# A streaming decode attention kernel: the critical section synchronised from GpSimd, and the last V blocks summed in three pieces instead of two

## The chip, the cores and the metric

The kernel runs on one core of one Trainium2 chip. Its time is the device time of one execution in microseconds (us).

## The reference, cut to what matters

```
# one token; x is [1, 1, 448]; 16 query heads, 8 KV heads, 65536 cached positions, head size 256
q = (x @ wq) -> 16 heads
scores = q . k_cache * 256 ** -0.5 ;  p = softmax(scores) ;  o = p . v_cache
a = o @ wo                                   # wo is [4096, 448]
b = gelu mixer of layernorm(x)               # small, with its own weights
out = g * a + (1 - g) * b                    # g = sigmoid(sum(x * gate_w))
```

K and V are 8 x 65536 x 256 numbers of 2 bytes each, 268 MB apiece. All of it must be read once. Everything else is small.

## The kernel before

K and V are walked in 48 chunks. SyncE issues all large loads in one queue, in a fixed order, each as soon as its buffer is free. VectorE transposes K blocks, TensorE forms scores and later the product with V, ScalarE takes the exponential. The whole kernel stands in one "critical" section: inside it the semaphores are the author's own; at its edges the framework lets one engine (here SyncE, by default) release the others at the start and collect a report from each at the end.

The change touches the last V chunk and these edges. The last chunk is cut into pieces, each with its own semaphore. The last 24 of its 80 blocks (a block is 64 KB) are summed "turned": two small matmuls per block that add straight to the finished product. Behind the V pieces come two loads of the last weights `wo`:

```
edges = [0, nlast - TURN - SB, nlast - TURN, nlast - TAIL, nlast]      # TURN = 24, TAIL = 10
for k in range(len(edges) - 1):
    lo, hi = edges[k] * DH, edges[k + 1] * DH
    sp.dma_start(out=vlast[:, lo:hi], in_=src[:, lo:hi]).then_inc(s_last[k], 16)
sp.wait_ge(s_oo, HKV - 1)
for r in range(2):
    ...                                                                # (cut) 224 KB each
    sp.dma_start(out=wo[:, r, :, :]..., in_=A_wo[at:at + DH, :]...).then_inc(s_wl[r], 16)
```

And what follows on TensorE (PE) and VectorE (DVE), up to the store:

```
pe.wait_ge(s_last[2], 16);  turned(edges[2], edges[3])                 # 14 blocks, 28 matmuls
pe.wait_ge(s_last[3], 16);  turned(edges[3], edges[4]).then_inc(s_fp, 1)   # 10 blocks, 20 matmuls
dve.wait_ge(s_fp, 4);       heads().then_inc(s_fd, 1)                  # oT
pe.wait_ge(s_fd, 3)
for k in range(4):
    r, cc = divmod(k, 2)
    if cc == 0:
        pe.wait_ge(s_wl[r], 16)                                        # each half needs its own wo load
    ...                                                                # (cut) 4 matmuls of the output projection
...                                                                    # (cut) copy the result; SyncE stores it
pool.wait_ge(s_out, 16)                                                # GpSimd waits for the store
```

The softmax here doesn't subtract the row's maximum and nothing guards it: scores larger than these inputs give would overflow.

## Time and profile before

| what | value | read from |
|---|---|---|
| time | 1265.84 us, median of 6 (1265.68 to 1266.03) | executions |
| DMA | 431 GB/s over the whole span, 9 tenths busy or more in nearly every slice | page, slices |
| TensorE / VectorE busy | 57% / 53% of the span | page, first part |
| end of the chain | last V piece lands at 1259.01, then 1.9 us of work | chain of waits |

The page of the kernel before: the busy shares, and then the span in 40 slices (tenths busy, then GB/s).

```profile
PE 718.4 (57%) x4296; PEld 275.5 (22%) x4296; DVE 675.1 (53%) x462; ACT 50.1 (4%) x127; POOL 78.5 (6%) x111
DMA  9999999999999999999999999999999999999998
GB/s 405 427 434 433 438 438 422 439 435 431 439 430 428 436 433 438 435 428 433 434 434 438 430 434 434 429 439 427 434 442 429 434 434 432 436 433 430 439 433 354
```

No compute engine is near full; the load queue is. The Trainium skill, "DMA: Bandwidth & Descriptors", section Specifications, gives a fabric ceiling of 435 GB/s for the 16 DMA engines of a core, and the 431 GB/s here agree with it (433 GB/s between 100 and 1200 us; the slices scatter around that, up to 442). Only what lies before the first load and after the last landing can change the time without changing the stream.

The chain of waits of the kernel before, its last pieces: start in us, length in us, what.

```profile
1229.03 29.98 DMA kbuf<-in_A_v_cache_dram
1259.01 0.04 issue
1259.05 0.69 PE misc L751 x20
1259.74 0.02 issue
1259.77 0.17 DVE oT L550
1259.94 0.04 issue
1259.98 0.60 PE acc L800 x13
1260.58 0.02 issue
1260.61 0.28 DVE res L807
```

By this view the last V piece (issued at 1229.03, landed at 1259.01) releases 20 turned matmuls, then `oT`, then the output projection. It suggests that a smaller last piece shortens the chain. But the view merges the 16 matmuls of the projection (it counts 13 of them) and names what released the first. The timeline shows the same, again with both halves of the projection in one line.

```profile
1259.05 0.68 PE L751 MATMUL misc<-pT,kbuf 128*128 128x2 bf16 x20 [0.21 <-DMA kbuf<-in_A_v_cache_dram]
1259.77 0.16 DVE L550 TENSOR_TENSOR oT<-misc,rden 128x4 bf16<-128x4 f32 x1 [2.82 <-PE misc L751]
1259.98 0.56 PE L800 MATMUL acc<-wo,oT 128*1 128x112 bf16 x16 [0.25 <-DVE oT L550]
1260.61 0.28 DVE L807 CAST res<-acc 97x112 bf16<-97x112 f32 x1 [0.68 <-PE acc L800]
1260.91 0.66 SPq L810 DMA_DIRECT2D out_dram<-res  x1
```

The records under these lines tell more. Eight matmuls start between 1259.985 and 1260.044, nothing for 150 ns, and eight more from 1260.194. The second `wo` load landed at 1260.152, 42 ns before. So the second half already waited for `wo`. No view reports it as idle time, because the modelled ends of the first eight matmuls (up to 1260.34) cover the gap. The view of DMA issues (size, median us from issue to landing) shows the two loads; they were issued at 1229.51 and 1229.98:

```profile
kbuf<-in_A_v_cache_dram SPq DMA_DIRECT2D x1, 640.0 KB, 30.0
wo<-in_A_wo_dram SPq DMA_DIRECT2D x2, 224.0 KB, 30.1
```

The start, from the timeline of the kernel before:

```profile
0.90 0.52 ACTq L90 DMA_DIRECT2D x_row<-in_A_x_dram  x1
0.94 0.10 POOL L269 MEMSET ident<- 14x14 bf16 x1 [0.50 <-SPq L815]
0.96 0.39 SPq L90 DMA_DIRECT2D vbuf<-in_A_wq_dram  x1
```

GpSimd is released by SyncE (`<-SPq L815`, the edge of the section), and SyncE's first load of the stream is issued at 0.96 us.

### The profile page before, as it was taken

How to read it: one execution, taken by the hardware profiler on the slowest of the kernel's cores; microseconds unless marked ns; L12 is line 12 of the kernel's file. 1: busy time of each engine (PE TensorE's matmuls, PEld its weight loads, DVE VectorE, ACT ScalarE, POOL GpSimd, SP SyncE). 2: the span in 40 equal slices, each digit the busy share in tenths (PEclk: the TensorE clock that was granted, in tenths of full speed). 3: DMA queues.
4: the chain of work that ended last, by engine and by line, in shares of the span. 5: the costliest groups of instructions: out<-in, count | busy, mean ns of one | idle time of the engine just before them, and what ended most of it. 6: DMA issues, size and time to landing. Idle time of an engine off the chain costs nothing. (4 is left out here: it accounts for less than half of the span.)

```text
span 1263.6 us, 10623 instructions
## 1 busy us (share of the span) xinstructions
PE 718.4 (57%) x4296; PEld 275.5 (22%) x4296; DVE 675.1 (53%) x462; ACT 50.1 (4%) x127; POOL 78.5 (6%) x111
## 2 busy tenths in 40 slices
PE   4855655466554665456555565555645656456556
PEld 1311222122221222112221221222212222122212
DVE  5745555465544555455455555464545645465544
ACT  0000000000000000000000000000000000000000
POOL 1001010110110101101111011000000000000000
PEclk9987878778777788778877788777887788777877
DMA  9999999999999999999999999999999999999998
GB/s 405 427 434 433 438 438 422 439 435 431 439 430 428 436 433 438 435 428 433 434 434 438 430 434 434 429 439 427 434 442 429 434 434 432 436 433 430 439 433 354
DMA packets 16840, 544.30 MB, mean 431 GB/s; under 512 B 1856, under 2 KB 3906, under 8 KB 4290
## 3 DMA queue, kind: packets, MB, share of 16 engines
q1 hardware_dynamic: 16744, 544.22, 99.7%
q8 instruction: 2, 0.03, 0.0%
q10 hardware_dynamic: 90, 0.01, 0.0%
q14 instruction: 4, 0.03, 0.0%
HBM read 544.22 MB, written 0.00 MB: 431 GB/s over the span
## 5 line engine op out<-in xcount | busy, mean ns | idle before, releaser
L661 PE MATMUL sc<-kT,qw 128*128 128x512 bf16 x2048 | 571.8, 437 | 488.7 <-PEq L657 488.7
L532 DVE STREAM_TRANSPOSE kT<-kbuf 128x2048 f32<-128x2048 f32 x256 | 572.8, 2285 | 331.7 <-DVEq L524 331.7
L661 PEld LDWEIGHTS sc<-kT,qw 128*128 128x128 bf16 x2048 | 210.4, 108 | 848.7 <-issue 695.5
L675 PE MATMUL pv<-vbuf,pT 128*4 128x512 bf16 x2008 | 120.9, 389 | 27.1 <-PEq L705 26.8
L543 DVE TENSOR_TENSOR og<-pv,og 128x512 f32<-128x512 f32 x40 | 27.7, 692 | 98.8 <-DVEq L524 98.6
L608 ACT ACTIVATE p_t<-sc 128x512 bf16<-128x512 f32 x48 | 28.7, 597 | 1192.2 <-PE sc L661 1192.2
L675 PEld LDWEIGHTS pv<-vbuf,pT 128*4 128x4 bf16 x2008 | 47.2, 88 | 97.2 <-issue 51.7
L589 DVE STREAM_TRANSPOSE pT<-p_t 128x512 bf16<-128x512 bf16 x32 | 22.8, 711 | 74.4 <-DVEq L524 74.4
L635 POOL TENSOR_SCALAR t_b<-t_b 128x448 f32<-128x448 f32 x14 | 7.9, 564 | 360.6 <-ACT t_b L617 360.6
L639 POOL TENSOR_SCALAR t_b<-t_b,hw 128x448 f32<-128x448 f32 x14 | 8.9, 638 | 332.7 <-ACT t_b L625 332.7
L579 DVE STREAM_TRANSPOSE pT<-p_t 128x512 bf16<-128x512 bf16 x8 | 5.7, 711 | 26.9 <-DVEq L524 26.9
L644 POOL TENSOR_TENSOR ymix<-ymix,t_b 128x448 f32<-128x448 f32 x14 | 16.1, 1148 | 1.1
L643 POOL TENSOR_TENSOR t_b<-t_b,u_b 128x448 f32<-128x448 f32 x14 | 15.8, 1126 | 1.2
L638 POOL TENSOR_TENSOR t_b<-t_b,u_b 128x448 f32<-128x448 f32 x14 | 15.8, 1126 | 1.2
L720 PE MATMUL acc<-wo,oT 128*1 128x448 bf16 x28 | 7.9, 413 | 12.7 <-PEq L717 12.7
L542 DVE COPY og<-pv 128x512 f32<-128x512 f32 x8 | 5.5, 692 | 16.1 <-DVEq L524 16.1
L594 DVE STREAM_TRANSPOSE pT<-p_t 128x512 bf16<-128x512 bf16 x8 | 5.7, 711 | 14.9 <-DVEq L524 14.9
L617 ACT ACTIVATE t_b<-h_bc,b1T,w1T 128x448 f32<-128x448 f32 x14 | 10.5, 747 | 0.0
L631 POOL TENSOR_SCALAR u_b<-h_bc,w1T,b1T 128x448 f32<-128x448 f32 x14 | 10.0, 715 | 4.1 <-DVE hw L428 2.7
L608 ACT ACTIVATION_READ_ACCUMULATOR p_t<-sc 128x1 f32 x48 | 9.3, 194 | 0.0
L452 PE MATMUL sc<-vbuf,xw 128*128 128x512 bf16 x32 | 9.2, 456 | 0.0
L685 PEld LDWEIGHTS misc<-mask,og 128*128 128x128 f32 x64 | 8.7, 196 | 2.0 <-DVE og L543 0.9
(86 smaller groups left out, 77.3 us busy)
## 6 DMA issues: line engine op xcount, KB each, us to landing
kbuf<-in_A_k_cache_dram SPq DMA_DIRECT2D x32, 5120.0 KB, 33.2
vbuf<-in_A_v_cache_dram SPq DMA_DIRECT2D x31, 5120.0 KB, 20.6
kbuf<-in_A_k_cache_dram SPq DMA_DIRECT2D x16, 6144.0 KB, 35.5
vbuf<-in_A_v_cache_dram SPq DMA_DIRECT2D x16, 6144.0 KB, 23.8
wo<-in_A_wo_dram SPq DMA_DIRECT2D x7, 448.0 KB, 23.6
vbuf<-in_A_wq_dram SPq DMA_DIRECT2D x1, 3072.0 KB, 10.3
kbuf<-in_A_v_cache_dram SPq DMA_DIRECT2D x1, 2560.0 KB, 25.3
kbuf<-in_A_v_cache_dram SPq DMA_DIRECT2D x1, 1024.0 KB, 27.2
```

The lines of the kernel that those rows point to most:

```text
L452: last = e.matmul(q_ps[:], lhsT=xw[:, k, HKV - 1 - n:HKV - 1 - n + 128], rhs=rhs, start=(n == 0 and k == 0), stop=(n == HKV - 1 and k >= K ...
L532: dve.transpose(out=kT[b][:].bitcast(FP32), in_=kn[:, s * SB * 128:(s + 1) * SB * 128]).then_inc(s_kt, 1)
L543: return dve.tensor_tensor(out=og[:], in0=pv[:], in1=og[:], op=ALU.add)
L589: dve.transpose(out=pT[:], in_=p_t[:]).then_inc(s_pt, 1)
L608: ins = act.activation(out=p_t[:], in_=sc[:], func=ACT.Exp, scale=scale, accum_out=den[:, c:c + 1])
L617: ins = act.activation(out=t_b[:], in_=h_bc[:], func=ACT.Square, scale=w1T[:, b:b + 1], bias=b1T[:, b:b + 1],)
L631: lambda: pool.tensor_scalar(out=u_b[:], in0=h_bc[:], scalar1=w1T[:, b:b + 1], scalar2=b1T[:, b:b + 1], op0=ALU.mult, op1=ALU.add,),
L638: lambda: pool.tensor_tensor(out=t_b[:], in0=t_b[:], in1=u_b[:], op=ALU.mult),
L643: lambda: pool.tensor_tensor(out=t_b[:], in0=t_b[:], in1=u_b[:], op=ALU.mult),
L644: lambda: pool.tensor_tensor(out=ymix[:], in0=ymix[:], in1=t_b[:], op=ALU.add),
L661: ins = pe.matmul(sc[:], lhsT=qw[:, q, at:at + 128], rhs=kv[:, :, q // 2, :, q % 2], start=(first and q == 0), stop=(last and q == 7), ski ...
L675: ins = pe.matmul(pv[32 * a:32 * a + 4, :], lhsT=pT[:, k, :, ROW0 + s], rhs=vt[:, j * DH:(j + 2) * DH], start=first and k < 4, stop=last a ...
```

## The change

Its intent: GpSimd, which in any case gives the start barrier's release and waits for the store, should also release and close the section, without its drain; and fewer turned matmuls should be left when the last V piece lands.

```diff
-TAIL = 10
+TAILS = (10, 4)
...
-        edges = [0, nlast - TURN - SB, nlast - TURN, nlast - TAIL, nlast]
+        edges = [0, nlast - TURN - SB, nlast - TURN] + [nlast - t for t in TAILS] + [nlast]
...
-        pe.wait_ge(s_last[2], 16)
-        turned(edges[2], edges[3])
-        pe.wait_ge(s_last[3], 16)
-        turned(edges[3], edges[4]).then_inc(s_fp, 1)
+        for k in range(2, len(edges) - 1):
+            pe.wait_ge(s_last[k], 16)
+            ins = turned(edges[k], edges[k + 1])
+        ins.then_inc(s_fp, 1)
...
-    with tc.tile_critical():
+    with tc.tile_critical(sync_engine=mybir.EngineType.Pool, no_gpsimd_drain=True):
```

## The prediction

> **What bounds it.** The load stream. The page's slices show the 16 DMA engines at 9 tenths from start to end, 431 GB/s mean over the span (544.3 MB; the Trainium skill, "DMA: Bandwidth & Descriptors", Specifications, puts the fabric ceiling at 435 GB/s; this trace agrees). PE is busy 57%, VectorE 53%. The chain of waits is one DMA (the last V piece, 29.98 us from issue to landing at 1259.01) and then 1.9 us of work. So only start, tail and end can move, by tenths of a us in 1266.
>
> **The tail (sum in three pieces).** From the timeline: last V piece (10 blocks, 640 KB) lands at 1259.01; its 20 turned matmuls take 0.69; oT ends 1259.93; the output projection starts 1259.98 in two halves; result 1260.88; store issued 1260.91. With pieces of 6 and 4 blocks only 8 turned matmuls follow the last landing. One starts every 26 ns, so oT comes 12 x 26 ns = 0.31 us earlier. But the trace's landing records put the two last wo loads, queued behind V, at 1259.60 and 1260.15, and the second half of the projection starts at 1260.19, 42 ns after its weights: it waits for wo already, not for oT. No byte leaves the queue, so the second wo load lands no earlier; one more transfer may delay it a little (640 KB took 1.58 us = 415 GB/s, 224 KB took 0.55 and 0.59 us against 0.53 at 431 GB/s: an estimate of 0.02 to 0.06 us per transfer). The first half of the projection moves from 1259.98 to about 1259.65, the second half stays. Gain on the critical path: 0; estimate +0.03 us. The extra issue (0.43 us on SyncE) is hidden: it is issued 30 us ahead of landing.
>
> **Start.** The sequencer records show SyncE giving the release of the section at 0.72 us, the others branching on it at 0.76 to 0.82, the first load issued at 0.96. GpSimd gives the barrier's release at 0.61 and can follow at 0.69 (its spacing is 78 ns), so the first load may be issued about 0.05 us earlier, and the whole stream with it: -0.05.
>
> **End.** Before: the store's semaphore is complete at 1262.555; GpSimd branches (1262.58), drains (1262.74, only 41 ns), SyncE passes it on (1262.81, 1262.88, 1262.94), and the closing barrier starts at 1262.975. The other engines had reported at 1261.66 to 1262.04, while the store was in flight. After: the order of instructions shows that GpSimd first waits for the store, then releases the others, they drain and report, and GpSimd collects in three steps of some 75 ns before SyncE may enter the barrier. So a round that was hidden behind the store's flight moves behind it; the removed drain was 41 ns. Estimate +0.15 to +0.2 us.
>
> **Sum.** -0.05 + 0.03 + 0.17 = +0.15 us: 1266.0 us, range 1265.0 to 1266.9. Chances: faster by over 2% 0.005, within 2% 0.99, slower by over 2% 0.005.
>
> **What would show it.** Right: last V piece landing and 8 matmuls behind it instead of 20; first half of the projection at about 1259.65, second still some 40 ns after the second wo landing, PE idle between; DMA slices unchanged; store's completion to last instruction longer than the 1.04 us of before (about 1.2). Wrong: the second half of the projection moving up with oT; the second wo landing more than 0.1 us earlier; the end getting shorter.
>
> **What would make it wrong.** The stream's rate: 0.1% is 1.3 us, more than all terms together, and a different landing lag of the slowest DMA engine (0.7 us behind the middle ones in the last loads) could hide or fake an effect of this size. The GpSimd drain may cost more than its record shows.

## The result, and the profile after

The changed kernel took 1265.95 us (median of 6, 1265.88 to 1266.16), the kernel before 1265.84 us (median of 6, 1265.68 to 1266.03). The ratio is 1.0001, interval 0.9988 to 1.0014: the same. Ratios here are the mean time of one kernel's fast runs over that of the other's of the same rounds, so not quite the ratio of the medians. The means of the six are 1265.97 and 1265.85, with standard deviations of 0.10 and 0.14.

The changed kernel's slices (DMA busy, GB/s) are as before: the stream is untouched.

```profile
DMA  9999999999999999999999999999999999999998
GB/s 408 423 436 433 437 436 425 439 432 431 440 433 426 433 437 433 440 428 434 436 427 436 429 435 440 432 426 439 433 437 433 432 431 435 427 443 433 425 435 348
```

Its chain of waits, the last pieces:

```profile
1230.41 30.16 DMA wo<-in_A_wo_dram
1260.56 0.04 issue
1260.61 0.39 PE acc L800 x8
1260.99 0.02 issue
1261.02 0.28 DVE res L807
```

The last V piece has left the chain; the second `wo` load has taken its place, and the projection is now visibly in two halves. The timeline of the changed kernel shows both:

```profile
1259.41 0.37 PE L751 MATMUL misc<-pT,kbuf 128*128 128x2 bf16 x8 [0.19 <-DMA kbuf<-in_A_v_cache_dram]
1259.82 0.16 DVE L550 TENSOR_TENSOR oT<-misc,rden 128x4 bf16<-128x4 f32 x1 [2.81 <-PE misc L751]
1260.09 0.35 PE L800 MATMUL acc<-wo,oT 128*1 128x112 bf16 x8 [0.30 <-DVE oT L550]
1260.61 0.36 PE L800 MATMUL acc<-wo,oT 128*1 128x112 bf16 x8 [0.17 <-DMA wo<-in_A_wo_dram]
1261.02 0.28 DVE L807 CAST res<-acc 97x112 bf16<-97x112 f32 x1 [1.03 <-PE acc L800]
1261.32 0.65 SPq L810 DMA_DIRECT2D out_dram<-res  x1
```

From the last V landing to the end of `oT` the kernel before took 0.92 us (1259.009 to 1259.930), the changed one 0.62 us (1259.366 to 1259.982): 0.30 us less. It is all lost again in front of the second half, which starts 42 ns after its `wo` load in the kernel before and 44 ns in the changed one.

The start of the changed kernel, with SyncE's first load 0.07 us earlier (0.892 against 0.958 in the records) and GpSimd released by its own sequencer:

```profile
0.89 0.39 SPq L90 DMA_DIRECT2D vbuf<-in_A_wq_dram  x1
0.89 0.53 ACTq L90 DMA_DIRECT2D x_row<-in_A_x_dram  x1
0.97 0.10 POOL L269 MEMSET ident<- 14x14 bf16 x1 [0.53 <-POOLq L815]
```

The end is not in the views, which leave out drains and semaphore steps. The records of the engines' sequencers (their waits, branches and semaphore steps) show it. Times are starts in us, but ends for "is done" and for the last instruction; the store is complete at 1262.555 before, 1262.952 after:

```
kernel before                                      changed kernel
1261.62  SyncE releases the reports                1262.98  GpSimd's wait for the store ends
1261.66  ScalarE, VectorE, TensorE report          1263.13  GpSimd releases the reports
1262.04  SyncE's report is done                    1263.17  SyncE, ScalarE, TensorE, VectorE report
1262.58  GpSimd's wait for the store ends          1263.23  GpSimd reports
1262.74  GpSimd drains (41 ns) and reports         1263.32, .41  GpSimd collects, in two steps
1262.81  SyncE closes the section                  1263.50  GpSimd closes the section
1262.88, .94  SyncE enters the closing barrier     1263.53, .59  SyncE enters the closing barrier
1262.98  barrier starts                            1263.66  barrier starts
1263.60  last instruction ends                     1264.28  last instruction ends
```

Before, everything except GpSimd's own report happened while the store was in flight. After, GpSimd must first see the store, and then the whole round of reports runs. From the store's completion to the last instruction it is 1.04 us before and 1.33 us after.

So the two profiled executions differ by 0.68 us (spans of 1263.60 and 1264.28): 0.41 us because the second `wo` load landed later (1260.152 and 1260.563), 0.29 us at the end, and -0.01 us in between. The 0.41 us is more than the median times differ by. The two profiles are not of typical executions: the one before took 1265.38 us, the fastest for its kernel, the changed one 1266.16 us, the slowest of its six. Where the 0.41 us comes from is the second question for the experiments.

### The profile page after: what moved, and what is told of

It is laid out like the page before. It is cut to its first block, busy times and chain, and to the rows that moved or that the text cites. A ratio compares the mean times of both kernels' runs of the same rounds, so it can differ in the third digit from the quotient of the medians.

```text
span 1264.3 us, 10626 instructions
## 1 busy us (share of the span) xinstructions
PE 715.4 (57%) x4296; PEld 275.0 (22%) x4296; DVE 675.1 (53%) x462; ACT 50.1 (4%) x127; POOL 78.7 (6%) x111
```

## The experiments

The theory: the split (one more piece, so that 8 matmuls and not 20 follow the last V landing) saves its 0.3 us off the critical path (worth nothing), the start gains 0.07, the end loses 0.29; and the landing of the last load varies by some 0.5 us between executions of one kernel, because it is set by the slowest of 16 DMA engines, and something delays a different engine by a different amount in each execution. The rival: the split does gain 0.3 us, and the new synchronisation eats it.

All looks in one table. "wo late" is how far the last of the 16 landings of the second `wo` load (one for each DMA engine) comes after the ninth of them; all times in us. The expectations below quote some ends 0.02 us lower (1.02 and 1.31) than the records give (1.04 and 1.33).

| look | first load | last V lands | second wo lands | second half starts | store done to end | wo late |
|---|---|---|---|---|---|---|
| before | 0.96 | 1259.01 | 1260.15 | 1260.19 | 1.04 | 0.93 |
| before, again (state unknown) | 0.96 | 1259.27 | 1260.44 | 1260.48 | 1.04 | 1.18 |
| changed | 0.89 | 1259.37 | 1260.56 | 1260.61 | 1.33 | 1.30 |
| changed, again (state unknown) | 0.89 | 1259.27 | 1260.39 | 1260.44 | 1.33 | 1.24 |
| tail_only | 0.96 | 1259.49 | 1260.62 | 1260.66 | 1.04 | 1.35 |
| sync_only | 0.89 | 1259.15 | 1260.30 | 1260.35 | 1.33 | 1.19 |
| drain_kept | 0.89 | 1259.12 | 1260.23 | 1260.27 | 1.36 | 1.00 |
| store_on_sync | 0.89 | 1259.07 | 1260.19 | 1260.24 | 1.12 | 1.05 |
| store_on_act | 0.96 | 1259.22 | 1260.38 | 1260.42 | 1.05 | 1.03 |
| one_engine_free | 0.96 | 1260.67 | 1261.81 | 1261.86 | 1.04 | 2.61 |

### tail_only and sync_only: each half of the change alone

```diff
# tail_only: the changed kernel with
-    with tc.tile_critical(sync_engine=mybir.EngineType.Pool, no_gpsimd_drain=True):
+    with tc.tile_critical():
# sync_only: the changed kernel with
-TAILS = (10, 4)
+TAILS = (10,)
```

> Only the split of the last V piece (14, 6, 4); the section is synchronised from SyncE as before. Theory (the split is off the critical path, because the output projection's second half waits for the second wo load): 8 turned matmuls follow the last V landing, the projection's second half starts about 42 ns after the second wo landing, from the store's completion to the last instruction 1.02 us as before; time as before, 1265.84 plus 0 to 0.06 us. Rival (the split saves its 0.3 us, and the synchronisation from GpSimd ate it): about 1265.5 us.

> Only the synchronisation from GpSimd without its drain; the last V blocks in two pieces (14, 10) as before. Theory: first load issued at 0.89 us instead of 0.96, from the store's completion to the last instruction about 1.31 us instead of 1.02, sum +0.2 us: 1266.05 us. Rival (the split saved 0.3 us that this part ate): 1266.25 or more. Second rival (neither part does anything): 1265.84, with 1.02 us at the end.

Measured: tail_only 1265.86 us (1265.60 to 1266.04, 5 runs), sync_only 1265.94 us (1265.81 to 1266.24, 5 runs), the kernel before 1265.82 us (1265.47 to 1266.27, 9 runs) on the same chip. In tail_only 8 matmuls follow the last V landing, and the second half still starts with its `wo` load (1260.62 and 1260.66). Its chain of waits ends as that of the changed kernel:

```profile
1229.87 30.75 DMA wo<-in_A_wo_dram
1260.62 0.04 issue
1260.66 0.39 PE acc L800 x8
1261.05 0.03 issue
1261.07 0.27 DVE res L807
```

sync_only, with 20 matmuls behind the last V landing, has the first load at 0.89, the end of 1.33 us, and a second half that waits for `wo` as well (1260.30 and 1260.35). The rival wanted 1265.5 and 1266.25 us or more and falls, above all by the traces: the split alone gains nothing after the second `wo` landing, and the synchronisation alone has a start and an end that differ from before by what the records of the changed kernel say. The times alone would not have told so much: sync_only's median lies 0.12 us above the kernel before, inside the scatter of both; the means are 1265.87 (tail_only), 1266.01 (sync_only) and 1265.85 us (before), each with a standard error of 0.08 or 0.09.

Does the earlier start reach the end of the stream? The ninth landing of the second `wo` load averages 1259.18 us in the five looks synchronised from GpSimd and 1259.26 us in the five from SyncE. That fits the 0.07 us, but five looks of one kind scatter by 0.14 to 0.15 us, so it is not shown.

### wo_first_one and wo_first_split: is the split worth its 0.3 us where nothing hides it?

The two last `wo` loads are issued before the pieces of the last V chunk, so that V lands last. Once with V in pieces (14, 10), once in (14, 6, 4), both synchronised from SyncE.

```diff
+        sp.wait_ge(s_oo, HKV - 1)
+        for r in range(2): ... wo loads ...          # moved here
         for k in range(len(edges) - 1): ... V pieces ...
-        sp.wait_ge(s_oo, HKV - 1)
-        for r in range(2): ... wo loads ...
```

> The kernel before with the two last wo loads put ahead of the last V pieces, V in pieces (14, 10). Now the last V piece lands last, where the second wo load landed (about 1260.2 us), and nothing hides the 20 turned matmuls behind it. Expected for both theories: from the last landing to the projection's end 0.04 + 0.69 + 0.2 + 0.05 + 0.4 = about 1.38 us instead of 0.40; time 1265.84 + 0.95 = 1266.8 us. Its use is as the partner of the next run.

> The same with V in pieces (14, 6, 4). Theory (the split is worth 12 matmuls at 26 ns = 0.31 us, and the change could not show it because wo landed last): from the last landing to the projection's end about 1.07 us instead of 1.38, time 0.25 to 0.31 us below the partner. Rival (the split is worth nothing in any order, because a further transfer costs what it saves): from the last landing to the end unchanged, or the last landing later by as much.

Measured: 1267.02 us (1266.95 to 1267.13) and 1266.88 us (1266.57 to 1267.37), 5 runs each; ratios to the kernel before 1.0010 and 1.0009. The chain of waits of wo_first_one:

```profile
1229.14 31.45 DMA kbuf<-in_A_v_cache_dram
1260.59 0.05 issue
1260.64 0.70 PE misc L751 x20
1261.34 0.02 issue
1261.36 0.17 DVE oT L550
1261.53 0.04 issue
1261.58 0.57 PE acc L800 x10
```

and the timeline of wo_first_split, whose last V piece landed at 1260.50:

```profile
1260.54 0.29 PEld L751 LDWEIGHTS misc<-pT,kbuf 128*128 128x128 bf16 x8
1260.96 0.16 DVE L550 TENSOR_TENSOR oT<-misc,rden 128x4 bf16<-128x4 f32 x1 [2.78 <-PE misc L751]
1261.18 0.54 PE L800 MATMUL acc<-wo,oT 128*1 128x112 bf16 x16 [0.26 <-DVE oT L550]
```

From the last landing to the end of the projection: 1.53 us (1260.59 to 1262.12) and 1.22 us (1260.50 to 1261.72), so 0.31 us less, as the theory has it; both are 0.15 us longer than expected, since the 16 matmuls of the projection take 0.54 us when nothing parts them. The split is worth 0.31 us in the chain of this order and nothing in the order of the kernel, where `wo` lands last. The median times differ by 0.14 us only, less than the 0.25 to 0.31 us expected; the scatter of the split one (0.8 us between its slowest and fastest run) is too large to show 0.31. The order of the kernel before is the better one by 1.0 to 1.1 us (medians) in any case: in this kernel the last bytes should be those with the least work behind them.

### drain_kept, store_on_sync, store_on_act: what the end is made of

```diff
# drain_kept: the changed kernel with
-    with tc.tile_critical(sync_engine=mybir.EngineType.Pool, no_gpsimd_drain=True):
+    with tc.tile_critical(sync_engine=mybir.EngineType.Pool):
# store_on_sync: the changed kernel with
-        pool.wait_ge(s_out, 16)
+        sp.wait_ge(s_out, 16)
# store_on_act: the kernel before with
-        pool.wait_ge(s_out, 16)
+        act.wait_ge(s_out, 16)
```

> The changed kernel without the flag that leaves out the GpSimd drain. Theory: the drain is 41 ns and lies beside the other engines' reports, so end about 1.31 to 1.37 us, time 1265.95 to 1266.0 us. Rival (leaving out the drain is the gain of this change, and without it the new synchronisation is much slower): 0.2 us or more above the changed kernel.

> The changed kernel with one line moved: SyncE, not GpSimd, waits for the store. Theory (the end is longer because GpSimd both waits for the store and releases the round of reports, so the round starts only after the store): GpSimd now releases the round while the store is in flight, and the other engines report before it lands; from the store's completion to the last instruction about 1.05 us instead of 1.31, time 1265.95 minus 0.26 = 1265.7 us. Rival (GpSimd is simply slow at collecting, whenever the round starts): 1.2 us or more at the end, and no gain.

> The kernel before with one line moved: ScalarE, not GpSimd, waits for the store, the section synchronised from SyncE as before. Theory (what counts is which work is left after the store's completion, and GpSimd's branch and drain take 0.24 us of it): the same chain with a faster waiter, 0.95 to 1.04 us from completion to the end instead of 1.04; time 1265.75 to 1265.84, not to be told from before by its times. Rival (the waiter must be GpSimd because GpSimd closes the barrier): longer than 1.04.

Measured, from the store's completion to the last instruction: 1.36, 1.12 and 1.05 us, against 1.33 changed and 1.04 before. Times: drain_kept 1266.13 us (1265.86 to 1266.63), store_on_sync 1265.81 (1265.59 to 1266.29), both against 1265.82 before; store_on_act 1265.76 (1265.61 to 1265.96) against 1265.91 (1265.38 to 1266.25).

- The drain (46 ns in drain_kept, where it stands beside the other engines' reports) is worth 0.03 us of the end. Leaving it out is not what the change lives or dies by. The median time of drain_kept is 0.18 us above the changed kernel's, but the two were timed in different rounds and drain_kept with a spread of 0.8 us, so no more than those 0.03 us can be told.
- With SyncE waiting for the store, the records show GpSimd collecting its first pair of reports at 1261.01, 1.6 us before the store is complete (1262.60), and only SyncE's own report after it. That takes back 0.21 of the 0.29 us. The expected 1.05 us was too low by 0.07: GpSimd's steps in that chain are some 86 ns apart.
- With ScalarE as waiter under SyncE's synchronisation the end stays at 1.05 us: the chain has the same number of steps, and from the end of its wait to its report ScalarE took 0.156 us and GpSimd 0.161. The expected 0.95 to 1.04 us was missed by 0.01: ScalarE is no faster a waiter. The rival's "longer than 1.04" is met by that 0.01 us only, so the waiter need not be GpSimd.

### before_again, after_again, one_engine, one_engine_free: why the last landing moves

```diff
# one_engine_free: the kernel before, with eight more loads of 8 KB, each into one partition
+        for k in range(8):
+            act.dma_start(out=extra[k:k + 1, :], in_=A_k_cache[0, 0, 16 * k:16 * k + 16, :]...).then_inc(s_x[k], 16)
...                                                                    # (cut) ScalarE waits for all eight only just before its first exponential
# one_engine (the failed first try): all eight into the same place, and after each of them
+            act.wait_ge(s_x, 16 * (k + 1))
```

> The kernel before, looked at a second time. Theory (which DMA engine the instruction fetches fall on, and so how late the slowest engine is, differs between executions of one kernel): first load at 0.96 us, store's completion to the last instruction 1.04 us, both to 0.02 us as in the first look, while the second wo load lands anywhere between 1259.9 and 1260.7 us (1260.15 in the first look). Rival (the 0.41 us between the wo landings of the two kernels is made by the change): 1260.15 to 0.1 us again.

> The changed kernel, looked at a second time. Theory: first load at 0.89 us and 1.33 us at the end, to 0.02 us as in the first look; the second wo load lands anywhere between 1259.9 and 1260.7 us (1260.56 in the first look). Rival: 1260.56 to 0.1 us again.

> The kernel before with eight extra loads of 8 KB into one partition, issued from ScalarE at about 13 to 40 us, if they run on one DMA engine each (the records will show). Theory (the loads are split over 16 engines in fixed shares and the queue never runs dry, so what delays one engine at the start is still missing at the end; this is what makes the scatter of some 0.3 us between executions): 64 KB more on one engine are about 2.4 us at the 0.309 us that 8 KB took in the instruction fetches; the last landing behind the median engine grows from about 1.0 to between 2 and 3.4 us, and stays so from 60 us to the end; time +1.2 to +2.4 us, 1267.0 to 1268.2. Rival (a late engine makes its lag good within the run): lag at the end about 1 us and time 1265.9.

> The earlier run with extra loads on one engine let ScalarE wait for each, which held up the whole kernel and let the load queue run dry, so it could not answer. Here the eight loads of 8 KB go to eight partitions and ScalarE doesn't wait for them. Theory (a lag of one engine stays to the end while the queue never runs dry): the last engine's landing behind the median is about 0.4 + 2.47 less the engine's own lead, so 2 to 2.9 us, at 70 us and still at 1258 us; the second wo load lands 1 to 1.9 us later than before; time 1266.9 to 1267.8 us. Rival (a late engine makes its lag good): about 1 us at the end, 1265.9 us.

Two kernels looked at a second time: the start and the end repeat to 0.01 us, the landing of the second `wo` load doesn't. It is 1260.15 and 1260.44 in two looks at the kernel before, 1260.56 and 1260.39 in two looks at the changed one. So the 0.41 us between the first two profiles was not made by the change. The landings tell what it is: those of the second `wo` load are spread over 1.4 us before and 1.8 us after, the ninth of the 16 comes at 1259.22 before and 1259.26 after, and only the last ones differ (0.93 and 1.30 us behind the ninth). The Trainium skill, "DMA: Bandwidth & Descriptors", section "Why a DMA increments its semaphore by 16 and not by 1", says that the engines of a DMA finish independently and each adds its own one; these 16 landings agree.

one_engine did not answer. Its waits held ScalarE until after 57 us, the first exponential came late (it waited 45.9 us for the extra loads), and the load queue ran dry: the third slice moved 311 GB/s instead of 434 in the kernel before. Its time was 1276.08 to 1282.17 us (4 runs, median 1281.61), far outside what either theory expected, for that reason. One thing can be read from it: the lag of the slowest engine (behind the ninth) was 2.20 us in the load that landed at 70.9 us, before the dry stretch, and 1.09 us in the next, at 93.5 us, after it.

one_engine_free keeps the queue full and takes 1267.00 us (1266.97 to 1267.05, 4 runs) against 1265.92 (1265.57 to 1266.03, 7 runs), ratio 1.0009; expected were 1266.9 to 1267.8 by the theory and 1265.9 by the rival. ScalarE is not held up: its first exponential starts at 44.55 us, against 44.53 before. Each extra load is one packet of 8 KB (0.31 us), and the eight are moved between 17 and 43 us. The last engine's lag behind the ninth grows from 1.10 us in the load that lands at 27 us to 3.09 us at 44 us; it is 2.80 us in the K load that lands at 72 us and 2.64 us in the last V piece, almost 1190 us later. The ninth landing of the second `wo` load is at 1259.21 us, as in the kernel before (1259.22): the middle of the engines lost nothing. The view of DMA issues has the last V piece and the last two `wo` loads 1.0 and 1.1 us later than before (30.0 and 30.1), as the earlier V pieces are too:

```profile
kbuf<-in_A_v_cache_dram SPq DMA_DIRECT2D x1, 640.0 KB, 31.0
wo<-in_A_wo_dram SPq DMA_DIRECT2D x2, 224.0 KB, 31.2
```

64 KB of 544 MB is 0.01% of the bytes and should cost 0.15 us at 431 GB/s if it were spread evenly; it cost 1.1 us. That is what loads split over 16 engines in fixed shares would do, when each engine works through a queue of its own and none runs dry: little evens out, and the slowest engine sets the last landing. The trace names no engine for a packet, so the fixed shares, and that all eight packets fell on one engine, are inferred: only the last landing stands far out (2.80 us behind the ninth at 72 us, the last but one 1.37). Nor is the lag kept exactly: from 44 us to the end it shrank by 0.5 us, and in the kernel before the spread from the first to the last landing went from 1.66 us at 42 us to 1.44 us at the end.

In the ordinary kernels the records show what can delay single engines: packets of instruction fetch. Near 30 us there is one of 16 KB (taking 1.0 to 1.2 us) and one of 8 KB (0.31 us), two of 8 KB follow between 274 and 324 us, one between 844 and 871 us, and a last one of 16 KB near 1258 us. Before the fetches near 31 us the last engine was 0.60 us behind the ninth in the kernel before, and 1.33 us in the load that landed at 42 us; in the changed kernel 0.58 and 1.67 us. In all eleven traces without extra loads the lag rises by 0.7 to 1.2 us between these two loads. In one_engine the fetch at 1267.24 (0.96 us) seems to have met the slowest engine: its lag went from 0.96 to 2.20 us between one V piece and the next. In the changed kernel the fetch at 1258.54 seems to have met another engine: only the second latest landing moved, from 0.38 us behind the ninth (first `wo` load) to 1.22 us (second). That the fetches make the scatter is thus seen in time order in several traces, but no run removed them: it stays inferred. That a delay made in the first 45 us is carried to the end is shown by one_engine_free.

No version here beats the kernel before by more than the scatter: the earlier start under GpSimd's synchronisation (0.07 us) comes with an end that is as much longer in its best form (0.07 us, store_on_sync).

## Why the prediction was right, point by point

- **Bound by the load stream.** Right; the slices are the same in both kernels.
- **The split saves 0.31 us off the critical path.** Right in size (0.30 us between the last V landing and the end of `oT`; 0.31 us in the pair with `wo` first) and in effect: the second half of the projection starts 42 to 45 ns after its `wo` load in every look of the table, and tail_only takes the time of the kernel before.
- **First half of the projection at about 1259.65.** Wrong in detail: it came at 1260.09, and at 1260.04 in the second look. The last V piece landed later in those executions (1259.37 and 1259.27 against 1259.01), and in the first look the half waited for the first `wo` load too (1259.95). The prediction took one execution's landings for fixed.
- **A further transfer costs 0.02 to 0.06 us.** Not settled: in the ordinary looks the second `wo` load landed at 1260.19 to 1260.62 with the split and at 1260.15 to 1260.44 without, and the lag of single engines hides so small a term.
- **Start -0.05 us.** Right: -0.066 us in the first load's issue.
- **End +0.15 to +0.2 us.** Right in mechanism (a round that was hidden behind the store's flight moves behind it; store_on_sync hides it again and gets 0.21 us back), mis-sized: it is +0.29 us. The prediction counted the collecting steps at 75 ns; they are 86 to 100 ns apart, and GpSimd's own release and report are two steps more.
- **Sum +0.15 us, 1266.0 us.** The medians differ by 0.11 us, the means by 0.115 us with a standard error of about 0.07 us (from the two standard deviations and six runs each). The measured terms add up to -0.07 + 0.29 = +0.22 us, plus whatever the further transfer costs. The times hold both; they can't tell 0.15 from 0.22, and hardly from 0. The prediction had the end 0.1 us too small and a cost of a transfer that no run shows, so that its sum lies so near the measured difference is in part luck; what is right in it are the directions of start and end, and that the split gains nothing.
- **A different lag of the slowest engine could hide or fake it.** Right: the later landing made 0.41 of the 0.68 us between the two profiles, and 0.37 of that is the last engine's lag (0.93 and 1.30 us behind the ninth landing; the prediction had put it at 0.7 us).

## What to carry to other kernels

Before shortening what follows the last transfer named by the chain of waits, look at what lands after it: a wait in the middle of a group of instructions doesn't show in a merged line, but the landing beside the start of each instruction does. An engine that waits for the last event should not also be the one that releases a round of reports: let the round run while the event is in flight. And in a kernel bound by one full queue over 16 DMA engines, the end is set by the slowest engine; a few KB on one engine early on can still be missing there (64 KB in the first 45 us cost 1.1 us here). The lag was 0.93 and 1.18 us in two looks at the kernel before, a difference as large as the effect under study, so look twice before explaining a difference between two profiles.

## What the Trainium skill lacked or had wrong

- "DMA: Bandwidth & Descriptors": it says that the engines of a DMA finish independently, but not that a lag of one engine is kept as long as the queue stays full. Here 64 KB on one engine gave a lag of 2.80 us at 72 us and 2.64 us at the last V landing (1260.67), and 1.1 us of time.
- "Runtime: NRT & Kernel Launch", Instruction fetch mechanics, calls the cost of crossing a 16 KiB block of instructions "mostly hidden". For the sequencer that may hold; beside a full load queue a fetch of 16 KB occupies a DMA engine for 1.0 to 1.2 us, and in one run (one_engine) the last landing of the last V piece, just after such a fetch, was 1.24 us further behind the ninth than that of the piece before (2.20 and 0.96 us). That the fetch did it is inferred.
- No page gives the time of one step of such a round of reports, in which a sequencer waits for a semaphore and passes it on (the pages have only figures for parts, and for the runtime's own barrier). Here the steps are 78 to 100 ns apart on GpSimd and 60 to 72 ns on SyncE, and GpSimd's drain at the end of a section took 41 to 46 ns.
